# Another written order for TensorE's groups of matmuls (ORDER and LINE) in a four-layer transformer kernel

## The chip, the cores and the metric

The kernel runs on one core of one Trainium2 chip. A core has four compute engines that run side by side, each through its own list of instructions: TensorE (PE in the profile; its weight loads are listed apart as PEld), VectorE (DVE), ScalarE (ACT) and GpSimd (POOL). SyncE (SP) issues most of the transfers (DMA) between the chip's main memory and the on-chip memory. The engines wait for one another through semaphores.

The metric is the device time of one execution, in microseconds (us): 1479.94 before, the median of three runs (1478.99 to 1480.87). Lower is better.

## What is computed

Four layers are applied to 2048 tokens of width 448: A, B, A, B. A is an attention whose memory goes from segment to segment; B is a gated product (GLU). In short:

```python
def _A_ref(x, mem0, Wq, Wk, Wv, Wo, seg_len):     # seg_len 32, M 8 memory rows, 16 heads of 256
    mem = mem0
    for s in range(n_seg):                        # 64 segments
        xs = x[:, s * seg_len:(s + 1) * seg_len, :].copy()
        h = jnp.concatenate([mem, xs], axis=1)    # 40 rows
        q, k, v = ...                             # h times Wq, Wk, Wv
        p = _softmax(jnp.where(mask, q k / 16, -1e9))
        o = p v Wo
        mem = o[:, :M, :].copy()
        outs.append(o[:, M:, :])

def _B_ref(x, W_gate, W_up, W_down):
    gate = x W_gate
    h = gate * (gate > 0) * (x W_up)
    return h W_down

x = x + _A_ref(_layernorm(x), ...)
x = x + _B_ref(_layernorm(x), ...)
x = x + _A_ref(_layernorm(x), ...)                # the same weights again
x = x + _B_ref(_layernorm(x), ...)
```

The eight memory rows of a segment need those of the segment before it. So there is a recurrence of 63 steps in each A layer that can't be cut into parallel pieces.

## The kernel before, in words

**Weights first.** The kernel folds Wq with Wk into a matrix A and Wv with Wo into a matrix B, head by head. For this TensorE transposes the loaded weights (L864) and multiplies them (L880); the results go to A and Bsb. The code handles eight pairs of heads; the loads of each pair are issued on SP's queue (function `load`, with `weights` and `values` around it), those of Wq and Wk first, then those of Wv and Wo.

**The recurrence (`chain`, `middle`).** One pass of the main loop is a step; step n computes the memory rows of segment n of the first A layer and, seven steps behind (LAG = 7), those of segment n - 7 of the second. A step on TensorE is: memory times A (L1063), scores (L1296), then after the softmax on VectorE and ScalarE the transposes of the probabilities (L553 or L547), their product with the rows (L1357 and L1360), the product with B (L1107, in three groups; in the first two steps another form at L1200 to L1222), and the sum of the partial results with a selection matrix Sel (L533 with Sel, or L1139). Between these, VectorE, ScalarE and GpSimd take results out of the PSUM banks, split them in a high and a low part (Ohi and Olo, L1117 to L1122), turn them and write the next step's inputs.

**The rest fills in.** Everything else has slack: the 32 other rows of each segment, done for a tile of 128 tokens at a time (`att_group`: L1445 for the product with A, L1471 scores, L553 or L547 transposes, L1357 and L1360, then L533 or L537 for the product with B), the layer norms (`norm`, L1377 to L1390, transposes through L533), the GLU (`glu_units`, L1548 and L1577, and `glu_down`, through L533 or L537), and the stores. 

**How the order is made.** Every piece of work is an operation of a small planner, `_Sched`. Each has the engines that it may run on, a cost, what it reads and writes, and a priority. The planner goes through time, gives each engine its next operation and each result a PSUM bank (2 of pool C, 6 of pool G), and then writes the engines' instructions with the waits that the dependences need. Two strings steer it:

- LINE gives TensorE's order outright, for 2244 groups of matmuls. All groups stand in a list in program order; each sign is the place (0 to 79, and `~` adds 80) of the next group to take out of what is left:

```python
left = [o for o in self.ops if "pe" in o.engs]
...
out.append(left.pop(k + SIGNS.index(c)))
```

- ORDER holds a sign for each of 1132 parts of the program. It shifts the priority of that part's operations on the other engines and on SP's queue, in quarters of a step from -6.5 to +6.5:

```python
self.shift = 0.25 * (STEPS.index(ORDER[self.unit]) - 26) if self.unit < len(ORDER) else 0.0
```

Operations of the recurrence (level 0) are not shifted. Among the operations that could start, an engine takes those of the recurrence first and then the one with the lowest shifted time.

Three things follow from TensorE's order. Some groups have more than one form (`also`): the product with B and the down product of the GLU as full-array matmuls or in four strips of 32 columns (L533 or L537), transposes as full-array matmuls or in two row halves (L553 or L547). `line` picks the form that a group's neighbours have. A group whose form differs from the one before it is a turn. And where the planner sees TensorE idle for over 300 ns, `filler` puts matmuls that compute nothing used (L1613).

Of the kernel before, what the change touches and what calls it, by code (L numbers as in the profile page):

```python
# [32 lines left out]
ORDER = ("ICaaaaOUrUDzaqcLWBFvhKAQmXFbHJff0ZK0wA0bEK0NDJXhjQmlgNYQnskhcpNJDHZNZngWZTjmcjBAjxHSSfuazSiaMjVabyVardZaAxxvaa"
         "EaYgAaJrzaDcdaw0soaarpGhuNovjusPpyoeuyUBGJkuJFzJGx0tKaaacQaiNFmxXLyHxb00ADnzLBabRixTkKxGdaJXaIoicaqRaeuGFjpisL"
         "FcxuhjeZZv0CLUpBgeqL0egdRFyA0DaAAadPinsdymSWAiFrACcmGYxLcpcHvEYPmNEhvSTxPGnUaKl0PoPFoZjqPpXLmLLkPtatKanladLuBM"
         "vVacjOdMMa0bRkhDsXuevuhUWgFWUJjUAIAdYtapPaptYXDbGqNwcqAMiufAdvneygyexTpgEuIzKOjduGyWNv0dwbjgkuWyUPgaklsRtAapJZ"
         "SBaaxZazOryqpAViKovTklti0IkpHXIpCHjQFzEEzebgLcvAjkpGFaDHaoQGQc0xvLbnoJCpyUSXNrfYKuOeUuuOjUmQKAumJrdwbUtRGmfffc"
         "uZuF0NBYiiXwpK0pkpazCaxgSLIcYopEQzmNdxygZUdLlXHALQIuiGnZXcucuuLAWQVJavJahWrFbhnXTYBHOyHywgrOLPvYdBDuTsQyjlJrcR"
         "ZkxHGgVdoexoYmXmVBcxcGGhdcIbXxMsmaXBaoDGpL0GYgLn0SAPPyaQPdHWVJAIRjxdQGQOS0UXKlgtyObaEhaPtvBWTAJIoDZelscyxSCcds"
         "ndERVDSsrqvXOgYAswzuiyvgPiSf0UWjJuZHdBTrcN0fuOZyanhaIkEz0EsdGNyptHWTl0SiWCcQdqUiDEGQNYAlfmbPcLiwZoalTarMGlVdZb"  # L40
         "DLaVgRUWmanPhdttSUYlvNDDVxsTNNBcavVfpUveDiBzVtXxHjIREbnnpTzkYpcaYRaDmZaeaLlWPNozCKEe0SKUdfTzAxPrxdTEKbDqBfBXyx"
         "saANaasOtPpFycdVRiQYBzqmpHFQwUAWWepGzOGyGrRGIzIKYmpfzie0jHVsWhwCfuCtIAqAy0reaggzaMaoen0arBEurDaaaaaaTlneKDPaaa"
         "aaaaaaaaaaaaaaaaPEcWONgzaTGfZbfY")
# [55 lines left out]
class _Sched:  # L99
# [107 lines left out]
    def line(self):  # L207
# [1541 lines left out]
```

## Time and profile before

| | |
|---|---|
| median of three runs | 1479.94 us |
| lowest and highest | 1478.99 and 1480.87 us |
| the profiled execution | 1480.49 us |
| its span, first to last instruction | 1478.7 us |
| granted TensorE clock | 1.000 |
| DMA, mean over the span | 23 GB/s |
| in the first two fortieths of the span | 279 and 149 GB/s |

How to read the profile. One execution is taken by the hardware profiler. Times are microseconds unless marked ns. A row of a group or of the order in time names the line of the code (often a helper's: all results taken out of PSUM by `copy_any` have L523 or L526, all transfers L821), the engine, the operation, the tile written and the tiles read (buffer numbers are left out, so psG stands for any bank of pool G), the shape, and how many instructions were merged (x). In the rows in order of time the first two numbers are the start and the length; what stands in brackets is the engine's idle time before it and what ended that. A row of a wait names who waited for whom, the total, how often, and the longest. A row of busy times by stage has the stage, its length, then for PE, PEld, DVE, ACT and POOL the busy time and the number of instructions, and last the granted clock, the share of the DMA engines, and GB/s. Matmuls are pipelined: one of 448 columns is listed with some 350 ns, while the next can start 189 ns after it. So a busy PE is not a PE at its peak, and how closely matmuls follow is read from their starts.

### The profile page before, as it was taken

What the parts mean: (1) busy time and instruction counts of PE and PEld (TensorE: products, weight loads), DVE (VectorE), ACT (ScalarE), POOL (GpSimd) and SP (SyncE); (2) the same over time, 40 slices, a digit from 0 to 9 for tenths busy, and PEclk for the clock granted to TensorE, in tenths of its full rate; (3) what the DMA queues carried; (4) which work ended last, traced back from release to release, by engine and by line L of the source; (5) the groups of instructions that cost most, each with busy time, mean ns of one, the idle gap of its engine ahead of it and who ended that gap; (6) DMA issues with size and microseconds to landing.
All of it is one profiled execution on the core that took longest, in us unless ns stands there. A gap on an engine that the chain in (4) does not pass through costs nothing.

```text
span 1478.7 us, 82785 instructions
## 1 busy us (share of the span) xinstructions
PE 1467.1 (99%) x36957; PEld 1044.7 (71%) x36957; DVE 1131.3 (77%) x3703; ACT 909.4 (62%) x2632; POOL 175.7 (12%) x681
## 2 busy tenths in 40 slices
PE   9999999999999999999999999999999999999999
PEld 6656766777767776777768667677668676777676
DVE  7657778788878778687877778588876878788775
ACT  7775666676656656565656657466655656565543
POOL 3011111111111111011110111011110111011000
PEclk9999999999999999999999999999999999999999
DMA  9402100000000000000000000000000000000000
GB/s 279 149 26 71 51 8 9 8 9 8 9 5 14 9 14 9 3 19 5 18 5 14 9 14 9 4 18 5 16 6 14 7 11 12 5 11 5 11 6 15
DMA packets 62260, 34.09 MB, mean 23 GB/s; under 512 B 31808, under 2 KB 61776, under 8 KB 61904
## 3 DMA queue, kind: packets, MB, share of 16 engines
q1 hardware_dynamic: 61584, 28.54, 7.6%
q8 instruction: 290, 4.75, 1.3%
q14 instruction: 66, 0.54, 0.1%
q10 hardware_dynamic: 320, 0.26, 0.1%
HBM read 21.36 MB, written 1.84 MB: 16 GB/s over the span
## 4 chain that ended last, share of the span: by engine, by line
PE 96%; DVE 2%; ACT 1%; DMA 0%; issue 0%; SPq 0%; POOL 0%
PE psG L533 17%; PE psG L1445 17%; PE psC L1107 9%; PE psG L1548 9%; PE psC L1063 7%; PE psG L537 6%; PE psG L1063 5%; PE psG L1107 3%; PE psG L880 3%; PE psG L1357 3%; PE psG L1577 3%; PE psG L1471 3%; PE psC L1357 1%; PE psC L1296 1%; PE psG L864 1%; PE psC L1445 1%
## 5 line engine op out<-in xcount | busy, mean ns | idle before, releaser
L1445 PE MATMUL psG<-HT,A 64*128 64x128 bf16 x4932 | 279.5, 216 | 1.2 <-issue 1.1
L1445 PE MATMUL psG<-HX,A 64*128 64x128 bf16 x3699 | 262.1, 216 | 0.0
L1445 PEld LDWEIGHTS psG<-HT,A 64*128 64x128 bf16 x4932 | 231.0, 94 | 12.8 <-issue 5.2
L533 PE MATMUL psG<-Bsb,P 128*128 128x448 bf16 x909 | 194.2, 353 | 0.0
L1445 PEld LDWEIGHTS psG<-HX,A 64*128 64x128 bf16 x3699 | 191.3, 94 | 0.2 <-issue 0.2
L523 ACT ACTIVATE Ug<-psG 64x128 bf16<-64x128 f32 (+2 forms) x433 | 152.3, 370 | 55.4 <-PE psG L1445 43.3
L1280 DVE STREAM_TRANSPOSE uT<-Usb 128x384 bf16<-128x384 bf16 x280 | 144.5, 536 | 0.0
L1107 PE MATMUL psC<-Bsb,YTm 128*32 128x448 bf16 x2800 | 142.3, 353 | 0.1
L1063 PE MATMUL psG<-A,mT 64*32 64x448 bf16 x4088 | 134.3, 350 | 0.3 <-issue 0.2
L1548 PE MATMUL psG<-GG,glu 64*128 64x256 bf16 x2324 | 133.8, 269 | 0.0
L526 DVE CAST Ug<-psG 64x128 bf16<-64x128 f32 (+2 forms) x278 | 116.6, 429 | 17.9 <-PE psG L1445 12.3
L1063 PE MATMUL psC<-A,mT 64*32 64x448 bf16 x3752 | 125.8, 350 | 0.3 <-DVE mT L526 0.3
L533 PEld LDWEIGHTS psG<-Bsb,P 128*128 128x128 bf16 x909 | 78.7, 97 | 64.7 <-issue 5.6
L1548 PEld LDWEIGHTS psG<-GG,glu 64*128 64x128 bf16 x2324 | 110.1, 94 | 16.4 <-issue 1.9
L523 ACT ACTIVATE P<-psG 128x448 bf16<-128x448 f32 x207 | 106.6, 545 | 9.1 <-PE psG L1360 8.0
L1107 PEld LDWEIGHTS psC<-Bsb,YTm 128*32 128x32 bf16 x2800 | 71.2, 97 | 55.2 <-DVE YTm L526 0.7
L526 DVE CAST P<-psG 128x448 bf16<-128x448 f32 x148 | 89.2, 614 | 8.8 <-PE psG L1360 7.9
L1063 PEld LDWEIGHTS psC<-A,mT 64*32 64x32 bf16 x3752 | 62.1, 92 | 46.4 <-DVE mT L1145 4.4
L1063 PEld LDWEIGHTS psG<-A,mT 64*32 64x32 bf16 x4088 | 69.1, 92 | 30.2 <-issue 2.5
L526 POOL COPY HR<-Rsb 8x96 bf16<-8x96 bf16 (+1 forms) x132 | 37.2, 281 | 438.7 <-ACT Rsb L523 336.7
L1558 ACT ACTIVATE P<-psG 128x512 bf16<-128x512 f32 x83 | 49.4, 596 | 61.4 <-PE psG L1548 51.8
L1559 DVE TENSOR_TENSOR P<-P,psG 128x512 bf16<-128x512 bf16 x83 | 56.6, 682 | 36.4 <-ACT P L1558 36.1
(283 smaller groups left out, 3192.8 us busy)
## 6 DMA issues: line engine op xcount, KB each, us to landing
HR<-xn SPq DMA_DIRECT2D x128, 32.0 KB, 1.9
Tsb<-Rsb SPq DMA_DIRECT2D x256, 1.5 KB
Tsb<-Rsb SPq DMA_DIRECT2D x256, 2.0 KB
Bsb<-in_A_Wq_dram SPq DMA_DIRECT2D x6, 384.0 KB, 6.5
Bsb<-in_A_Wk_dram SPq DMA_DIRECT2D x6, 384.0 KB, 5.3
HR<-Rsb SPq DMA_DIRECT2D x126, 1.5 KB
HR<-Rsb SPq DMA_DIRECT2D x126, 2.0 KB
X<-in_A_x_dram SPq DMA_DIRECT2D x16, 112.0 KB, 3.8
```

The lines of the kernel that those rows point to most:

```text
L523: return E.activation(out, i, ACT.Copy, scale=1.0 if scale is None else scale)
L526: return E.tensor_copy(out, i)
L533: return E.matmul(out, lhsT=lhsT, rhs=rhs, **k)
L537: i = E.matmul(out[q], lhsT=w, rhs=rhs, tile_position=(0, 32 * j), **k)
L1063: i = E.matmul(ub[v].ap()[32 * j:32 * j + 32, 0:D], lhsT=self.mT[rw, WHERE[b], first:first + 32], rhs=cols, start=(b == 0), stop=(b == 6), ...
L1107: x = E.matmul(bk.ap()[32 * j:32 * j + 32, c0:c0 + d1 - d0], lhsT=self.YTm[:, q, :], rhs=self.Bsb[:, chunks[q], d0:d1], start=(i == 0), st ...
L1280: self.s.add("dve", 560, busy=486.0, fn=lambda E, e, q=q, of=of: E.transpose(outs[:, q], of), r=[("Usb", 2 * half + v, g) for v in vs for ...
L1357: return E.matmul(ps[:, n * q - off:n * q + n - off], lhsT=HR[rows, 128 * q:128 * q + 128], rhs=PT, start=True, stop=True, tile_position=( ...
L1445: i = E.matmul(ub[v].ap()[:, 128 * n:128 * n + 128], lhsT=self.A[rw, b, a0:a0 + 128], rhs=HT[rw, WHOLE[b], :, 0:SEG] if CROSS[b] is None e ...
L1548: i_ = E.matmul(two[v].ap()[:, 256 * c:256 * c + 256], lhsT=self.Wgu[rw, b, f0:f0 + 128], rhs=self.GG[rw, :, WHOLE[b] if CROSS[b] is None ...
L1558: s.add("act", ev_cost(512)["act"], lambda E, e, dst=dst, z=z: E.activation(dst, z(0), ACT.Relu), r=[two[0]], w=w, room=old)
L1559: s.add("dve", dv_cost(512), lambda E, e, z=z, dst=dst: E.tensor_tensor(dst, dst, z(1), ALU.mult), r=[two[1]], w=w)
```

## The change

Both strings are replaced, and nothing else. Both LINE strings place 2238 groups and leave the last six to program order; the old one has six `~` among its signs, the new one four. The functions that read the strings, the operations with their costs, tiles and dependences, the forms a group may have, and the buffers are the same. The first steps follow an older order, and the rest was searched on from there by the same rules. The two strings begin and end so:

```diff
-ORDER = ("ICaaaaOUrUDzaqcLWBFvhKAQmXFbHJff0ZK0wA0bEK0NDJXhjQmlgNYQnskhcpNJDHZNZngWZTjmcjBAjxHSSfuazSiaMjVabyVardZaAxxvaa"
...
-         "aaaaaaaaaaaaaaaaPEcWONgzaTGfZbfY")
+ORDER = ("wNaaaakeXaHRFRltlLTThvTInfRKLKSbzAOjIyTuXpvkWFDhFTTBurfhuDrlyVNFIDsnQWCkUOrPojWEKoQnmZqxjvoaVOjaaTQaApoaBNphaa"
...
+         "aaaaaaaaaaaaaaaanJmDaNxRaMcLybRh")
...
-LINE = ("AAAACAKABAIHAFEBBBAAHHAADABBABAIHBDAABAAAAIHBBBABAAAAIHHCFAACBAAH*HCDAABAABAIHCFBDAAAJAAKHGBDDABAAFIAhAddAcABA"
...
-         "APWJDDIHKAAANADFAFEABAEAAHDCAAAAADCBFAHEFEAD")
+LINE = ("AAAACBKBBIIACCBCBAAAHHEFBBBBABAJIBEAACBABAHICDCCAAAAAJHABBBCBABAIHCFBCCAAAAHIDFCABAAJBAHJBEFEBAAAAfjgAffACFABA"
...
+         "WEIDIHAJAAAACKECADCAKADADCAAAAADBBFAGEEEEE")
```

The signs of ORDER for the loads of Wv and Wo, for the eight pairs in the code's order (parts 82 to 89), are shifts of -4.75, -2, -2, 1.25, 5, 0, 6.25, -2 before and -2.5, 3.25, 3, -0.25, 4, 5.75, 2.25, 5.25 after.

More of the change, by code (lines that the diff above doesn't have):

```diff
@@ L32 @@
 STEPS = "ABCDEFGHIJKLMNOPQRSTUVWXYZabcdefghijklmnopqrstuvwxyz0"
-ORDER = ("ICaaaaOUrUDzaqcLWBFvhKAQmXFbHJff0ZK0wA0bEK0NDJXhjQmlgNYQnskhcpNJDHZNZngWZTjmcjBAjxHSSfuazSiaMjVabyVardZaAxxvaa"
[L34 to L42, printed above, removed]
-         "aaaaaaaaaaaaaaaaPEcWONgzaTGfZbfY")
@@ new lines @@
+ORDER = ("wNaaaakeXaHRFRltlLTThvTInfRKLKSbzAOjIyTuXpvkWFDhFTTBurfhuDrlyVNFIDsnQWCkUOrPojWEKoQnmZqxjvoaVOjaaTQaApoaBNphaa"
+         "baXiTaivDaCZCaVPHdaaEGAvjNKtOdjPUuqaByLiWIhuYTZmDL0NkaaaFDaoOlOvXSnPFy0neYWFLBLyAcxcIdoOLaBGRvMANasraKTJPRpHb0"
+         "LLxi0HhOZycEIBpvAGiwEexrCniStBahPaEiEwFdiUDNsiBHRItmfgNUqpidqNDnhNBXegTYhwdcjylLTrTWoUglJwXohXglKGadLaBJGGzuUq"
+         "umucUAYHyaNkmvvDoj0EXhOlceFAUIBHnxTxKmaISaKvxOVbdZfEjqAFnLAACtYuOgPGsSRGRcTWKzjXoKCSbm0y0JqHpudEhCUaTqlXrADaeT"
+         "PFaatDaLpVnhpsqRiqvGymkG0DzzgbIrcSGBzutzKergZXdAAkuwxaATaRkAvY0KoBAeoRPfzcSDUmGgKoTNxVeqyAXQdAHwePLiKUzVOkcNfT"
+         "QewM0KJS0pXspOrYneaJlaAEbPOcKXdujzVzSrggFoWsQXfYwRjQFehKXsuFhxxfP0g0aBVarnIxThVNLxiHlXpJugbMXQkYmhFjnRHyyTJPcp"
+         "JggyASVpNKfxemnARIrxSUcVecolCIkVSagzaFlRwd0cA0iS0LdEpPan0GRSVMmqvHRxVNgOt0NbOjYtunKaAdahtjVQThbpfVZxorrOxUjzik"
+         "nXCqWaIlzlmXigQEacgwayTSQXfB0BuaSfZtqfZkcIsWfxSYaZNamzWzHEDngEIpGzBpS0JSKAzQEVCvXXQPsPAkfGdbnnaNvgaYSauDeYtduW"
+         "qDQVQauMUadmViHtahFCelfuPTsgNkRZePkLpICYvMEzzzgxDjBiNxqnqGR0YRgafSaoEbmTatQl0JoTRTGL0krpWkTlAjGfWEjfXbPqmTjZdp"
+         "iaURawQryepunYDqRfqSKxqfVkrdwZAieIyRYIRyLrqMTQmyUmGKxTE0ZdpSehGHwM0thAtsFwTwaCVFaqXeNF0LgMriIiaaaaaabLmNKToaaa"
+         "aaaaaaaaaaaaaaaanJmDaNxRaMcLybRh")
@@ new lines @@
+SIGNS = "ABCDEFGHIJKLMNOPQRSTUVWXYZabcdefghijklmnopqrstuvwxyz0123456789+-*/=<>()[]{}.,:;!"
+LINE = ("AAAACBKBBIIACCBCBAAAHHEFBBBBABAJIBEAACBABAHICDCCAAAAAJHABBBCBABAIHCFBCCAAAAHIDFCABAAJBAHJBEFEBAAAAfjgAffACFABA"
+        "ZTAqXAEMASSA~VAQAPAlOABALAAZJCAKAGGAFBAaVAC-CABAWaFBEADPAECMDAEQLKAAESEOOOADEKDAIDCABBDABAAXAAAMADAAAHVNASaAFX"
+        "AFENHAAAEEHMBAZFYYYY>FIWAAUATFFRRRAAPAROOOAAALAAJoJvJAIIAHBJGGGAAEAACABAAAAXAAOUaAAAAWKdAJaJMRAWMAKHAAAJEJIAZD"
+        "AXXXXCCCUaCEABQACOAAQMMMAAKAKKKKJx5QJA1IIDLHHHAGGGGGGABEAJDACAAAAABRABAANTAAAXWAcJGASIAGVJAFAAGFDDAFAJZZZZBDAC"
+        "AETAAXRCCPAANNNOAALALLLL87LAQvJJCIBHHHIAGGGGGGfAFAKADACAAEAAACAAOUAAAAXeeKVLKAZSM}vMdAcAqKAAFAEEHASDA33FkECzGA"
+        "BYBuzAtlCjCGoooAAmAEVDmkkUAgAMflBBVcBAaZ7IYYYILAVCKVVVJAASAAANUOAMMgGLLLMjGGJAKLKbUJAPXIdHbHiHNAXKAKKJFFFAADDr"
+        "rrFQFFDmAUMGoAhAFf;EHdddAAbAcdcFEAAAXVAAUZTTAARRR4AQtSSSBEEBAAALAAAGHMAGFgFFFIAFADAABODBBZYRLnBVKzKZBYBLtLLBBB"
+        "FQKBEJI)>>BDDAC-CCECA6-X5AccBB000AAyAA0yyQvcRtbsATwgAAnDmqDckkkHDiJAgAAeeeWAAHALYeAAAVEDxYwTGlWGjGQQQAAOAOOOGL"
+        "AcKATJPEcIbIiMIIIAAGAzzzZFBQ2vADATrDCpAoooE~ConBnnnADkCAioADAfCCdAEbbbAAZZIDCXXXAAAbUAARRvRlRRRARnRGAABAAAJAAV"
+        "AaAfTelUkFAbhAFDDNzACLNLCAKBzJMBBBFFBGhGnBPA+++CjcGC5-CC3ABA0rBAxxxAAvAwwwld1stAbPGooDsnAmmmAmAKKiCFghgAKAdVOh"
+        "Awava2aaaCCYCAAYYYEoDAcUdjUAEQAPEjOpOoDNNNAALEKAI222EUDGAxRA1EVtAsDDApppFp~CpoCFElllCASiFAADDjdAFAFZEAAWWWAAUA"
+        "AATTTzrASYvEBQOEAMMCAAAIIIAAAFAAAAYBQCkcjPECCXMMCbU6BBwB2LBBBJIoLBEJJ>(>BDoDACe>H8CCLAB3B2AjBByyyAAwAAwwwcjAtb"
+        "yq;PqFo}oOCmmmnAMkAjljjBChMmAfAeAAAbbbAAZCFEbZZCVWAAEaTbAARAPPGBBMMMAAKCtJI777IOO-4ANBA0AAZxQDvvvDDMGrAsssRGFI"
+        "ouAlAMjj!Gi,GGgggAAAdAeeecAEAAYDCWAAATAAWRmRRRAhRGCCBAALAJAAVAAAAXAQABiiODBBLVUBKZKBKPBJ0JBBBFFBGADDA=<=DmCdc9"
+        "FCAg-ZA3u2lC000AAyFgAxxxAeARtAqQ;pp,pQsAnnnBCBlkCOAiiiAAffAAAcAgHaRHYYYAAWCYZYXNUCAAARACAUOVNNaCMMMBULADRJpI44"
+        "4EdHDAzFAA2DvOuVDsssAAqArrrpJoAnCHAMpjAiA<ADfffAAdBBEAbbbDDAAAUVAATASRvumAUQQQAEADAMAAJEAWcACCCAAQlRQZZTfTXCPR"
+        "zyBDBBLtPLBSO3B2BLIBBBFFBAsGDA555FfEC1CWC4CxABAuWRRrrrs~GRqAARopoBEmscbkCjA<AgAjAieeeEEcGbbbASACXCABBTYASAsADP"
+        "PPnEDNAPPPFNeXAKJKQAIlIcIaEDGGGAkGHFAFFvttAEGApAAtnIAlNDCiiiAAgDIeAgeed{DCAaEAAXcCWCAUUUAASAASSyqZARmGDPNCMMBL"
+        "LLABAIAdWAGAAnnSEdEjQaQEEXRAAABAMM1AsAyAAAKEEADA==hGFC+eABF*6BAE3mD111XAAzyFAxxAAAVtbQrhppQsAYsmmmDBBjPChlkAgA"
+        "hqnBeEeAccAbbbcAAAYYFPFYYAWHAAaTRAZJQZAOO4SOOOQExONAWV8CATZADAYQCGOvOOOAAMFLOOAFEIKAAIGBFFAEEEAEACAQBAdJHASAQA"
+        "WEIDIHAJAAAACKECADCAKADADCAAAAADBBFAGEEEEE")
```

19 lines of the change are left out of this document (removed).

## The prediction

> **What bounds the kernel now.** I read the page first, then the busy time by stage, then TensorE's own waits, then three places in order of time.
>
> ```profile
> span 1478.7 us, 82785 instructions
> PE 1467.1 (99%) x36957; PEld 1044.7 (71%) x36957; DVE 1131.3 (77%) x3703; ACT 909.4 (62%) x2632; POOL 175.7 (12%) x681
> ```
>
> TensorE (PE) is busy for 1467.1 of 1478.7 us, so 11.6 us are idle in all. The change adds and removes no matmul of the computation. What it can win is the idle time, the filler matmuls that the planner writes where it foresees a gap, and the cost of going from one tile form to another. The stages say where this lies (the second number is PE's busy time):
>
> ```profile
> 0.00:100.00 100.00, 96.55 (x1588) 61.22 (x1588) 66.28 (x158) 75.94 (x150) 20.00 (x62) 1.00 0.57 161
> 100.00:200.00 100.00, 98.77 (x2503) 67.60 (x2503) 75.00 (x257) 61.39 (x192) 13.43 (x54) 1.00 0.19 52
> 200.00:310.00 110.00, 108.39 (x2950) 75.72 (x2951) 88.50 (x305) 72.39 (x227) 17.71 (x73) 1.00 0.05 10
> 310.00:500.00 190.00, 189.99 (x5069) 136.98 (x5066) 153.61 (x520) 118.28 (x358) 22.17 (x87) 1.00 0.04 9
> 500.00:1000.00 500.00, 499.57 (x13193) 362.84 (x13187) 384.18 (x1279) 308.44 (x921) 56.43 (x222) 1.00 0.05 11
> 1000.00:1479.00 479.00, 473.83 (x11679) 340.38 (x11672) 363.76 (x1189) 272.98 (x788) 45.93 (x183) 1.00 0.04 10
> ```
>
> The first 310 us hold 3.45 + 1.23 + 1.61 = 6.3 us of idle time, the next 690 us only 0.01 + 0.43 = 0.4, the last stage 5.2. Of the last stage some 3 us are the end itself, which the order of groups can't reach: the last DVE addition starts at 1475.78, and a store follows.
>
> ```profile
> 1474.54 2.22 SPq L821 DMA_DIRECT2D out_dram<-X  x2
> 1475.78 0.62 DVE L1530 TENSOR_TENSOR X<-psG,X 128x448 bf16<-128x448 f32 x1 [1.27 <-PE psG L533]
> ```
>
> ```profile
> PE psG L880 <- ACT Bsb L523: 1.4, 5, 0.4
> PE psG L1445 <- issue: 1.1, 2, 0.8
> PE psC L533 <- DVE Olo L1122: 0.6, 2, 0.3
> ```
>
> PE's own waits are short and spread: 1.4 us on weight products, 0.6 us in the recurrence, and 1.1 us of "issue", in which it waited for nothing that the profile shows. The granted clock is 1.00 in every stage. So PE streams at full rate nearly everywhere, and one rewritten order can't be far from another.
>
> **The change part by part.** Each sign of LINE is the place of the next PE group in the list of those left, in program order. I read both strings off against that list of 2244 groups. 897 stand at the same place, half of all have moved by one place at most, one in ten by five or more. What every group computes is the same. Four things come out.
>
> *Tile forms.* Neighbours of unlike form (full array, four strips, two row halves and so on) are 543 before and 538 after. The price of a turn is in this stretch, which serves below too; it is step 10 of the recurrence:
>
> ```profile
> 235.15 1.12 PE L1107 MATMUL psC<-Bsb,YTm 128*32 128x448 bf16 x20
> ...
> 236.32 0.54 ACT L1117 ACTIVATE Ohi<-psC 128x448 bf16<-128x448 f32 x1 [0.54 <-PE psC L1107]
> ...
> 236.55 0.40 PE L533 MATMUL psG<-ident,xn 128*128 128x128 bf16 x4
> ...
> 236.79 0.73 PE L1613 MATMUL psG<-A 128*128 128x448 bf16 x3
> ...
> 236.90 0.62 DVE L1118 TENSOR_TENSOR Olo<-psC,Ohi 128x448 bf16<-128x448 f32 x1
> ...
> 237.56 0.20 DVE L1122 COPY Olo<-Olo 128x128 bf16<-128x128 bf16 x1
> ...
> 237.81 0.19 PE L533 MATMUL psC<-Sel,Ohi 128*128 128x32 bf16 x1 [0.29 <-DVE Olo L1122]
> ...
> 238.00 0.18 PE L533 MATMUL psC<-Sel,Olo 128*128 128x32 bf16 x1
> 238.11 0.09 PEld L1357 LDWEIGHTS psC<-PTr,HR 40*128 40x128 bf16 x1
> ```
>
> Eight 32-column matmuls start 237.81 to 238.00, 27 ns apart; the next group, of another form, loads at 238.11, so 0.11 us after the last start in place of 0.027: some 0.085 us a turn. Five turns fewer: **-0.4 us**. This holds under any cover, since PE pays it itself. Also 110 in place of 114 groups are in the four-strip form; its columns stream as long as the full form's (L1107 above: 20 matmuls in four strips in 1.12 us, that is five rounds of 0.19 and the pipeline's end), so nothing.
>
> *Step 10.* Here the step's last weight product (L1107) ends streaming near 236.1, ScalarE and VectorE make the high and low part of its sum (236.32 to 237.76), and only then can the Sel group start, at 237.81: a delay of 1.70 us. Before, 0.3 us of work stands between them, then three fillers (L1613) from 236.79. From 236.79 to 237.81 lie 1.02 us without useful work, and 0.23 before the xn transposes: 1.25 us. After, a group of 56 L1445 matmuls stands there, and the transposes behind it. Its price:
>
> ```profile
> 242.37 2.84 PE psG L1445 x98
> ```
>
> 29 ns each, so 1.62 us, and a turn: 1.7 to 1.8, just what the wait needs. The filler and the wait go: **-1.25 us** (0 if the L1445 group's own inputs came late, which no row here shows).
>
> *Step 1.* The same, among the weights' products:
>
> ```profile
> 77.41 0.27 PE L1296 MATMUL psC<-HT,uT 128*128 128x40 bf16 x4
> 77.52 0.35 PE L1613 MATMUL psG<-A 128*128 128x448 bf16 x1
> 78.24 0.55 PE L880 MATMUL psG<-P,glu 128*128 128x448 bf16 x2 [0.36 <-ACT Bsb L523]
> 78.99 0.23 PE L553 MATMUL psC<-ident,Pm 128*128 128x64 bf16 x2 [0.20 <-DVE Pm L1314]
> 79.42 0.55 PE L880 MATMUL psG<-P,glu 128*128 128x448 bf16 x2 [0.20 <-ACT Bsb L523]
> 79.91 0.34 PE L1357 MATMUL psC<-PTm,HR 40*128 40x128 bf16 x3
> ```
>
> By starts: 0.72 us from 77.52 to 78.24, then two matmuls of 0.19 and 0.37 lost to 78.99, then two of 0.03 and 0.37 lost to 79.42: 1.46 us. After, 42 L1445 matmuls (1.22 us) stand between the scores (L1296) and the transposes (L553), and the product that waited goes elsewhere. The softmax takes 78.99 - 77.52 = 1.47, of which 0.1 to 0.2 is left uncovered. **-1.3 us**; what is late next is the L1357 group, by about 0.1.
>
> *Step 9.* The change goes the other way here. The transposes L553 and their consumer L1357, with an L1445 group of 42 between them before, now stand side by side. Elsewhere that hop is seen without cover to spare:
>
> ```profile
> 429.37 0.22 PE L553 MATMUL psC<-ident,Pm 128*128 128x64 bf16 x2
> 429.62 0.22 ACT L523 ACTIVATE PTm<-psC 104x64 bf16<-104x64 f32 x1 [0.89 <-PE psC L553]
> 430.00 0.34 PE L1357 MATMUL psC<-PTm,HR 40*128 40x128 bf16 x6
> ```
>
> 0.63 us from start to start, less 0.06 of L553's own: **+0.57 us**. Queued behind it on PE are a GLU group and the next L553, which nothing else makes up for.
>
> Sum of what I can place: -0.4 - 1.25 - 1.3 + 0.57 = -2.4 us. Against it stands what I can't: an order that removes lates makes others, among queues of ScalarE and VectorE that I don't see. The covers of the common hops (L553 to L1357, L1107 to the Sel group, and so on) are about as short in one order as in the other, so a group is about as likely to come late. Bounds: none new (0), or as much again as all the idle time of the first 310 us (+6.3). I take +0.9, a third of the 2.55 relieved, because it is nearer to the short waits of the rows above than to a second stage's whole idle time. **Net -1.5 us.** The profiled execution took 1480.49 us (its span and 1.8 around it), 0.55 above the median of 1479.94; the difference put on the median gives **1478.4 us**.
>
> The "issue" gaps I leave as they are. [...]
>
> **Rivals.** *The relief stays and little comes anew (faster).* For it: the places above are exact, and the 690 us in the middle show that an order can leave 0.4 us idle. Then -2.4, with the 1.1 us of issue and part of the 1.4 us on L880 gone: -4.0, 1475.9.
>
> *Weights come late (slower).* ORDER also sorts the loads on SP's queue. The signs put the eight pairs of Wv and Wo in the order 0, 3, 6, 2, 1, 4, 7, 5 (by place in the code's list), where pair 1 was second. Its transposes (L864) stand seven places further down on PE, past the four L1063 groups of step 0, by the matmul counts some 4.4 us.
>
> ```profile
> GB/s 279 149 26 71 51 8 9 8 9 8 9 5 14 9 14 9 3 19 5 18 5 14 9 14 9 4 18 5 16 6 14 7 11 12 5 11 5 11 6 15
> Bsb<-in_A_Wv_dram SPq DMA_DIRECT2D x4, 384.0 KB, 6.4
> Bsb<-in_A_Wv_dram SPq DMA_DIRECT2D x8, 32.0 KB, 5.7
> P<-in_A_Wo_dram SPq DMA_DIRECT2D x3, 448.0 KB, 7.4
> 25.50 1.76 SPq L821 DMA_DIRECT2D Bsb<-in_A_Wv_dram  x3
> 47.15 1.06 PE L864 MATMUL psG<-ident,Bsb 128*128 128x128 bf16 x16
> ```
>
> A pair is 384 + 64 + 448 KB, 0.92 MB. The first starts at 25.50; four pairs ahead and 6.4 us to land must be over by 47.15 + 4.4 = 51.5. At the first slice's 279 GB/s a pair takes 3.3 us, and pair 1 lands at 45.1: no wait. At the second slice's 149 it takes 6.2, and it lands at 56.7, 5.2 us late: 1483.6. It decides below 0.92/4.9, 187 GB/s. Against it: that slice's mean counts the time after the last load, and semaphores may keep SP from the written order.
>
> *It does nothing.* Lates moved, none gained beyond the turns: -0.4 or so, 1479.5. This and my forecast fall together within the bound below.
>
> **How the numbers follow.** A change of this kernel's time under 0.2%, 3.0 us, can hardly be told from none. Forecast and "nothing", within 1477.0 to 1482.9: 0.45. Relief alone, or relief elsewhere too, below 1477.0: 0.35. Late weights 0.14, and scattered lates near the +6.3 bound 0.06, above 1482.9: 0.20. The likeliest case's own range is 1476.9 to 1481.5. The range for all reaches to the relief with 2 us more (1473.9) and to the late weights (1483.6): 1473.5 to 1484.0.
>
> **What would show it.** In the changed profile: no L1613 row near step 10 and an L1445 group before its first Sel matmul; an L1445 group between L1296 and L553 in step 1; PE's idle time before L1357 in step 9 near 0.57; PE idle in the first 310 us 4 to 6 us in place of 6.3, and under 1 us from 310 to 1000. Late weights would show as PE waiting for a DMA between 45 and 60 us. I am wrong if the middle 690 us gain more than 1.5 us of idle time, or if the first 100 us change by more than 2 us.

## The result, and the profile after

The changed kernel takes 1477.18 us (median of 14 runs, 1476.22 to 1478.09), the kernel before 1480.33 (14 runs, 1478.99 to 1481.37). The ratio is 0.9979, with a 95% interval of 0.9971 to 0.9987. That is 3.15 us less, which this interval tells from no change. Forecast were 1478.4 us and -1.5 us. The change is about twice the forecast one; the times lie closer because the kernel before is 0.4 us slower in these 14 runs than in the three that the forecast started from.

The profiled execution took 1478.07 us, and its span is 2.5 us shorter than that of before. The page, and the busy times by stage (stage, length, then busy time of PE, PEld, DVE, ACT and POOL; last the granted clock, DMA share and GB/s):

```profile
span 1476.2 us, 82695 instructions
PE 1465.7 (99%) x36911; PEld 1043.6 (71%) x36911; DVE 1127.7 (76%) x3723; ACT 905.1 (61%) x2610; POOL 175.9 (12%) x683
```

```profile
0.00:100.00 100.00, 97.51 (x1582) 61.15 (x1582) 68.81 (x169) 74.42 (x148) 20.34 (x64) 1.00 0.55 161
100.00:200.00 100.00, 99.19 (x2541) 68.52 (x2541) 74.32 (x254) 61.63 (x193) 13.89 (x54) 1.00 0.19 52
200.00:310.00 110.00, 108.06 (x2967) 75.74 (x2969) 86.80 (x305) 73.17 (x232) 18.59 (x76) 1.00 0.05 10
310.00:500.00 190.00, 189.10 (x5060) 136.47 (x5057) 150.14 (x514) 120.84 (x354) 20.63 (x82) 1.00 0.04 9
500.00:1000.00 500.00, 498.83 (x13119) 361.81 (x13111) 387.73 (x1296) 300.03 (x898) 56.22 (x223) 1.00 0.05 11
1000.00:1477.00 477.00, 472.99 (x11672) 339.86 (x11666) 359.86 (x1188) 275.05 (x790) 46.29 (x185) 1.00 0.04 10
```

TensorE is idle 2.49 + 0.81 + 1.94 = 5.2 us in the first 310 us (6.3 before), 0.90 + 1.17 = 2.1 in the next 690 (0.4 before), and 4.0 in the last stage (5.2 before). Part of the gain is not idle time at all: the fillers (L1613) near 7, 77 and 237 us are gone, and a filler counts as busy. From each one's start to the next group's start, they took 0.96 + 0.71 + 1.03 = 2.7 us before.

PE's waits (who waited for whom: total us, times, longest):

```profile
PE psG L1445 <- issue: 1.0, 2, 0.6
PE psG L1357 <- DVE PTm L526: 0.7, 1, 0.7
PE psC L1063 <- issue: 0.5, 1, 0.5
PE psG L1471 <- issue: 0.4, 1, 0.4
PE psG L880 <- ACT Bsb L523: 0.4, 2, 0.3
PE psC L533 <- DVE Olo L1122: 0.3, 1, 0.3
```

The waits on the weight products (L880) fell from 1.4 to 0.4 us, those in the recurrence (L533 on Olo) from 0.6 to 0.3. New is 0.7 at L1357, in step 9. "Issue" is still there, at other groups.

Where the time went is read best from the groups' starts. The same groups stand in both orders, so both traces can be asked when a given amount of TensorE's work was done. The difference (after minus before), summed from the start:

```
near, us of before    44    66   102   147   212   223   257   312   353   884   936  1459
difference, us      -0.1  +0.6  -0.6  -1.3  -1.6  -0.5  -1.6  -1.4  +0.0  -0.6  +0.2  -2.3
```

Step 9 (212 to 223) costs 1.1 and step 10 (223 to 257) gives 1.1. By 312 us the new order is 1.4 ahead, loses all of that by 353, and is 2.3 ahead near the end. The swings behind 312 us are for the most part at places of "issue", and the experiments turned on them.

### The profile page after: what moved, and what is told of

Same layout as the page of the kernel before. It is cut to its first block, busy times and chain, and to the rows that moved or that the text cites. A ratio compares the mean times of both kernels' runs of the same rounds, so it can differ in the third digit from the quotient of the medians.

```text
span 1476.2 us, 82695 instructions
## 1 busy us (share of the span) xinstructions
PE 1465.7 (99%) x36911; PEld 1043.6 (71%) x36911; DVE 1127.7 (76%) x3723; ACT 905.1 (61%) x2610; POOL 175.9 (12%) x683
## 3 DMA queue, kind: packets, MB, share of 16 engines
q8 instruction: 290, 4.75, 1.3%
## 4 chain that ended last, share of the span: by engine, by line
PE 96%; DVE 2%; ACT 1%; SPq 1%; issue 0%; DMA 0%; POOL 0%
PE psG L1445 17%; PE psG L533 16%; PE psC L1107 10%; PE psG L1548 9%; PE psC L1063 7%; PE psG L537 6%; PE psG L1063 5%; PE psG L880 3%; PE psG L1357 3%; PE psG L1577 3%; PE psG L1107 3%; PE psG L1471 2%; PE psC L533 2%; PE psC L1296 1%; PE psC L1357 1%; PE psG L864 1%
## 5 line engine op out<-in xcount | busy, mean ns | idle before, releaser
L1445 PE MATMUL psG<-HT,A 64*128 64x128 bf16 x4968 | 282.5, 216 | 0.1
L1445 PE MATMUL psG<-HX,A 64*128 64x128 bf16 x3726 | 264.5, 216 | 1.0 <-issue 1.0
L1445 PEld LDWEIGHTS psG<-HT,A 64*128 64x128 bf16 x4968 | 233.2, 94 | 11.8 <-issue 3.6
L1445 PEld LDWEIGHTS psG<-HX,A 64*128 64x128 bf16 x3726 | 193.0, 94 | 1.3 <-issue 1.3
L523 ACT ACTIVATE Ug<-psG 64x128 bf16<-64x128 f32 (+2 forms) x458 | 161.1, 369 | 51.5 <-PE psG L1445 34.7
L533 PE MATMUL psG<-Bsb,P 128*128 128x448 bf16 x862 | 184.9, 353 | 0.0
L1107 PE MATMUL psC<-Bsb,YTm 128*32 128x448 bf16 x2968 | 150.6, 353 | 0.0
L1063 PE MATMUL psG<-A,mT 64*32 64x448 bf16 x4116 | 134.7, 350 | 0.1
L1063 PE MATMUL psC<-A,mT 64*32 64x448 bf16 x3724 | 126.4, 350 | 0.9 <-issue 0.5
L526 DVE CAST Ug<-psG 64x128 bf16<-64x128 f32 (+2 forms) x271 | 110.7, 419 | 14.9 <-PE psG L1445 10.0
L523 ACT ACTIVATE P<-psG 128x448 bf16<-128x448 f32 x222 | 113.0, 545 | 10.0 <-PE psG L1360 7.2
L533 PEld LDWEIGHTS psG<-Bsb,P 128*128 128x128 bf16 x862 | 74.2, 97 | 61.7 <-issue 6.3
L1107 PEld LDWEIGHTS psC<-Bsb,YTm 128*32 128x32 bf16 x2968 | 75.7, 97 | 57.5 <-ACT YTm L523 0.7
L1063 PEld LDWEIGHTS psC<-A,mT 64*32 64x32 bf16 x3724 | 62.3, 92 | 49.0 <-DVE mT L1145 5.1
L526 DVE CAST P<-psG 128x448 bf16<-128x448 f32 x140 | 84.8, 614 | 11.1 <-PE psG L1360 10.5
L1063 PEld LDWEIGHTS psG<-A,mT 64*32 64x32 bf16 x4116 | 69.2, 92 | 28.4 <-ACT mT L523 1.5
```

The source lines that it names most:

```text
L523: return E.activation(out, i, ACT.Copy, scale=1.0 if scale is None else scale)
L526: return E.tensor_copy(out, i)
L533: return E.matmul(out, lhsT=lhsT, rhs=rhs, **k)
L1063: i = E.matmul(ub[v].ap()[32 * j:32 * j + 32, 0:D], lhsT=self.mT[rw, WHERE[b], first:first + 32], rhs=cols, start=(b == 0), stop=(b == 6), ...
L1107: x = E.matmul(bk.ap()[32 * j:32 * j + 32, c0:c0 + d1 - d0], lhsT=self.YTm[:, q, :], rhs=self.Bsb[:, chunks[q], d0:d1], start=(i == 0), st ...
L1445: i = E.matmul(ub[v].ap()[:, 128 * n:128 * n + 128], lhsT=self.A[rw, b, a0:a0 + 128], rhs=HT[rw, WHOLE[b], :, 0:SEG] if CROSS[b] is None e ...
```

## Experiments

Times are given as ratios to runs of the kernel before on the same chip, with 95% intervals, since its median differs by 1 us between groups of runs (1480.3 to 1481.3). Orders are read off LINE as a list of groups: line, number of matmuls.

### One place alone

Step 10's relief alone, and step 1's alone, each on the kernel before.

```diff
 L1357 x10
-L1445 x56
 L1445 x42
 L1296 x8
...
 L553 x2
+L1445 x56
 L533 x4
 L533 x8
```

> The kernel before with one group moved: the L1445 group of 56 matmuls that stood ahead of step 9's scores (210.7 us) is put behind step 10's last weight product (L1107) and the transposes, ahead of xn's (L533) and the Sel group. Theory A (the prediction: the move relieves step 10): step 10 gains 1.25 us, and step 9 pays nothing that it names: 1480.3 - 1.25 = 1479.1. Theory E (cover only moves: the 1.57 us of work taken from step 9 leaves a wait there of about the same size, by the fillers planned there 0.4 to 1.1 us): step 10 gains 1.0 to 1.25, step 9's scores or softmax wait 0.6 to 1.2 us more, in all 0 to -0.4 us: 1480.1.

```diff
 L1296 x4
+L1445 x42
 L880 x2
 L553 x2
...
 L1357 x5
-L1445 x42
 L1107 x20
```

> The kernel before with one group moved: the L1445 group of 42 matmuls that stood behind the L1357 group at 101.8 us is put behind step 1's scores (L1296, 77.4 us). Theory A (the prediction): step 1 gains 1.3 us and nothing is said of the place that it came from: 1479.0. Theory E (cover only moves): step 1 gains 0.8 to 1.2 us, and at 102 us the L1107 group or what stands ahead of it waits 0.5 to 1.2 us more: in all 0 to -0.4 us, 1480.1.

Measured: step 10 alone 1.0005 (0.9996 to 1.0014), no gain; step 1 alone 1.0015 (1.0006 to 1.0024), some 2 us slower. The filler at step 10 is gone, as is the one at 77.5 us. But in order of time (start, length, engine, line, tile written and read) the first kernel has, at step 9, with the scores that the moved group had covered:

```profile
212.22 0.55 PE L1613 MATMUL psG<-A 128*128 128x448 bf16 x2
212.96 0.36 PE L1296 MATMUL psC<-HT,uT 128*128 128x40 bf16 x8 [0.18 <-DVE uT L1280]
...
247.78 0.35 PE L1613 MATMUL psG<-A 128*128 128x448 bf16 x1
```

and the second, behind step 1 and at the place that its group came from:

```profile
80.18 0.73 PE L1613 MATMUL psG<-A 128*128 128x448 bf16 x3
81.30 0.55 PE L880 MATMUL psG<-P,glu 128*128 128x448 bf16 x2 [0.39 <-ACT Bsb L523]
...
103.78 0.36 PE L1613 MATMUL psG<-A 128*128 128x448 bf16 x1
104.46 1.32 PE L1107 MATMUL psG<-Bsb,YTm 128*32 128x448 bf16 x24 [0.31 <-ACT YTm L523]
```

The time in fillers rose from 6.4 us to 7.1 and 8.0. In step 1 the covered softmax was not even last: the product behind it (L880) waits for its evicted weights (Bsb) all the same. A group of L1445 is cover, and where there is no spare group, relieving one place uncovers another. For step 10 Theory E holds. For step 1 cover explains only a part. In its trace 0.85 us are lost before 66 us, where nothing was moved, some 0.5 between 66 and 110 us, and 3.1 behind 110 us, where both orders are the same; of these, waits for instructions make up 2.3 (6.7 against 4.4, below). The profiled execution was also the slowest of the 11. Nor is this move the whole trade of the change: the new order has a group of 56 at the place near 102 us again, and one group fewer in step 0 (that of 56 at 58.49 us before).

### The early half and the late half

Up to group 505 (about 304 us) and from there on, the two orders hold the same groups, so each can be continued with the other. In short (the kernel has the joined strings written out):

```diff
-LINE = OLD_LINE
+LINE = NEW_LINE[:505] + OLD_LINE[505:]
-ORDER = OLD_ORDER
+ORDER = NEW_ORDER[:262] + OLD_ORDER[262:]
```

(505 counts places: a sign with the ~ before it is one.)

> The new order for the first 505 of TensorE's groups (to about 304 us) and the first 262 places of ORDER, the old order for all behind. Theory I (the gain lies in the fillers and waits of the first 310 us; what the traces show behind that is chance of the fetch): the ledger of the first 310 us, -1.4 to -1.5, so 1480.4 - 1.5 = 1478.9, or with the start's part lower, 1478.5 to 1479.3. Theory J (half of it lies behind 310 us): 1478.8 as well here, but the next kernel tells them apart.

The other way round:

> The other half: the old order for the first 505 groups and 262 places, the new order behind. Theory I: only the turns of that part and chance, 1480.4 - 0.3 = 1480.1. Theory J (a later part with fewer dense runs of small matmuls waits less for its instructions in the mean): the traces' ledger there, -0.9, or what is left of the -3.15 beside the early half, -1.6: 1478.8 to 1479.5.

Measured: early half new 0.999 (0.9981 to 0.9999), late half new 0.9982 (0.9973 to 0.9991); the whole new order, beside them on the same chip, 0.998 (0.9971 to 0.9988). Of 1481 us that is -1.5 and -2.7; together they are more than the whole's -3.0, which the intervals allow. The early half agrees with the ledger's -1.4 at 312 us. The late half carries about as much or more, which the prediction did not see at all: Theory J.

### What the late half waits for

In the kernel before, the longest "issue" wait stands in the middle of a group of L1445 (a number in brackets is idle time, with what ended it):

```profile
1143.89 0.23 PE L1445 MATMUL psG<-HT,A 64*128 64x128 bf16 x2 [0.80 <-issue]
```

In the changed kernel the rows near 313 us show a group of 16 that stops after three matmuls:

```profile
312.76 0.37 PE L1296 MATMUL psG<-HT,uT 128*128 128x40 bf16 x8
312.97 0.23 PE L1471 MATMUL psG<-HT,Ug 128*128 128x40 bf16 x3
313.57 0.48 PE L1471 MATMUL psG<-HT,Ug 128*128 128x40 bf16 x13 [0.37 <-issue]
```

No tile comes new at the fourth. From the page, the larger of its two queues of the kind "instruction":

```profile
q8 instruction: 290, 4.75, 1.3%
```

4.75 MB over 290 packets is 16 KB a packet. The trace holds 74290 instructions of TensorE (36911 matmuls, as many weight loads and 468 others), that is 256 to a packet of this queue, and 127 matmuls (36911 over 290). And the two go together in time: when instruction 256k + 192 starts, k packets have landed, at 577 of 580 places in this trace and that of before. So I take this queue to load TensorE's program. Theory A below is that PE waits at packet boundaries, after stretches in which small matmuls use up instructions faster than they come.

First, the same stream with more instructions ahead (each 448-column filler as seven of 40 columns):

```diff
+            if ns > 100:
+                n, x = 7 * n, self.A[:, 1, 0:40]
             for _ in range(n):
                 i = E.matmul(self.psum[bank][:, 0:x.shape[1]], lhsT=w, rhs=x, start=True, stop=True)
```

> The changed kernel, with each filler matmul of 448 columns written as seven of 40 columns: the same time (7 x 27 ns for 190 ns), but 60 more matmuls, 120 instructions, in the stream by 301 us, so all later packet boundaries fall 60 matmuls earlier in the work. Theory A (fetch, in packets of 256 instructions): the wait inside the L1471 group near 313 us, after its third matmul, leaves that place and stands 60 matmuls earlier, at about the 27th matmul of the L1445 group near 310.6 us; that near 317.7 moves to the 30th matmul of the L1445 group before it, that near 898 to the 26th matmul of an L1063 group; their sizes may change; time 1477.2 within 1.5 us. Theory B (the wait belongs to the group, by its inputs or its bank): it stays after the third matmul of the L1471 group, and the time stays at 1477.2.

In its trace the L1471 group runs through, and the wait stands inside the L1445 group that starts at 315.30, after its 30th matmul:

```profile
315.30 0.23 PE L1445 MATMUL psG<-HT,A 64*128 64x128 bf16 x2
...
316.03 0.28 PE L1445 MATMUL psG<-HT,A 64*128 64x128 bf16 x4
316.76 0.23 PE L1445 MATMUL psG<-HX,A 64*128 64x128 bf16 x2 [0.45 <-issue]
```

This place was foretold to the matmul: 60 earlier in the work, the same count in the stream (7322). The other two places foretold, near 310.6 and 898 us, show no wait of 0.25 us or more in this profile. The time was missed: 0.9995 (0.9986 to 1.0004), some 2 to 3 us slower than the changed kernel, with more such waits (4.8 us behind 304 us in this profile, 3.8 in the changed kernel's). So in this run moving the boundaries was not free.

Second, two fillers more, one ahead of the wait, one where none follows soon:

```diff
-                n = int((t0 - free[e] - 300.0) * 0.8 / ns)
+                n = 3 if done in (516, 538) else int((t0 - free[e] - 300.0) * 0.8 / ns)
```

> The changed kernel with two more fillers of three 448-column matmuls (0.57 us each): one ahead of the L1296 group near 312.8 us, just before the wait in the L1471 group, and one ahead of an L533 group near 328 us, which no such wait follows for 13 us. Theory A (fetch): the first is absorbed, since the fetch goes on under it: the L1471 group's inner wait of 0.55 falls to about 0, and the groups behind come 0 to 0.15 us later; the second costs its 0.57 us, less what it saves of the 0.3 us near 341 us. In all +0.3 to +0.7: 1477.7. Theory B (a wait of the group itself, or chance): both cost 0.57 us: +1.1, 1478.3.

Its rows at the first place:

```profile
312.51 0.74 PE L1613 MATMUL psG<-A 128*128 128x448 bf16 x3
313.09 0.36 PE L1296 MATMUL psG<-HT,uT 128*128 128x40 bf16 x8
313.30 0.56 PE L1471 MATMUL psG<-HT,Ug 128*128 128x40 bf16 x16
```

The group runs through. The three fillers also move the packet boundary to the group's start, and the packet had landed 1.9 us before that. Against the changed kernel's trace the groups behind the first filler come 0.56 us later and 0.53 of it is back two groups on; a further 0.52 is won at the next wait (near 317.7). The second filler costs 0.57, and 0.30 is back at 341 us. So 1.14 us of useless work cost nothing that the runs can tell: 0.9973 (0.9964 to 0.9983), where both theories had expected some loss. The wait at 313 us is not in every profile (below), so one trace does not prove the repayment; that nothing was lost over nine runs supports it.

Third, the changed kernel once more:

> The changed kernel once more, unchanged, for a second profile of the same stream. Theory A with chance in the size (TensorE's stream is refilled in packets; the places of possible waits are fixed by the count of instructions, whether and how long it waits there differs from one execution to the next): inner waits only at the matmul counts 7195, 7322, 7958, 20691, 22604 of the first profile, or at others that are a multiple of about 127 matmuls away from these, with other sizes; all other waits (0.35 us at L880 near 52 us, 0.90 at step 9, 0.24 and 0.31 near 295 and 300 us) the same within 0.02 us. Theory H (all is fixed): the same waits with the same sizes. Time 1477.2 within 0.5.

Its second profile has the same dependence waits (0.35 us near 52, 0.90 at step 9, 0.24 and 0.31 near 295 and 300), while the inner waits differ in size and some in place. Counting the matmuls that started before each inner wait (one inside a group, 0.25 us or more), over these kernels and those of the next sections, these counts came up most often:

```
matmuls before it   seen in, us
 7195 to  7197      after 0.53, again 0.31, step 1 alone 0.48
 7322               after 0.51, again 0.30, short fillers 0.61, no fillers 0.65, late half 0.58
 7449 to  7451      short fillers 0.49, no fillers 0.65, step 1 alone 0.54, early half 0.28
20309 to 20312      before 0.50, again 0.91, four places 0.90, filler ahead 0.45, step 1 alone 0.60, early half 0.61
20691 to 20694      before 0.25, after 0.69, step 1 alone 0.52, early half 0.36
28840 to 28842      before 0.97, step 10 alone 0.42, step 1 alone 0.74, early half 0.55
28968 and 28969     before 0.35, step 10 alone 0.90, early half 0.26
```

Different orders, the same counts, about 127 or a multiple of it apart: in these traces the places go with the packets. Which of them wait, and how long, is partly chance (the wait at 20309 is 0.91 us in one profile of the changed kernel and under 0.25 in the other). So Theory A holds with chance in the size, and B and H fall.

The traces show it more directly, since they hold the arrival of each program packet. Take the twelve profiles of this and the other sections but for "One string without the other", behind 100 us, and count all of TensorE's recorded instructions (matmuls, weight loads, semaphore instructions). All 66 inner waits of 0.25 us or more stand at instruction 192 or 193 of a run of 256, and each ends 1.2 to 1.6 us after a packet has landed; at all packet boundaries together the median is 3.1 us. So, in these profiles, what such a wait is for is the next packet of the program.

A boundary can also fall at the start of a group, and then the profile may put the wait down to another engine. In the kernel before, one such wait stands at a packet boundary, 1.54 us after a packet landed:

```profile
1399.16 0.34 PE L1357 MATMUL psG<-PTx,HR 40*128 40x128 bf16 x6 [0.84 <-ACT Usb L523]
```

The weight loads of the same group stop with it, for "issue". The changed kernel has no wait there, and its lead grows by 0.8 us.

The chance in these waits has a mean, and the order changes it. Waits at groups that hold a packet boundary, over 0.1 us, summed behind 304 us (a group's time from its start to the next start, less the lower quartile of its kind):

```
old order there:  before 4.4, step 10 alone 4.9, step 1 alone 6.7, early half 4.1         mean 5.0
new order there:  after 3.8, again 2.6, late half 2.2, no fillers 2.7, filler ahead 1.6,
                  short fillers 4.8                                                       mean 2.9
```

2.1 us less in the mean, though one profile of the new order (short fillers) lies among those of the old. Against it stands a new wait for VectorE of 0.25 to 0.3 us behind the L1360 group near 1141.5 us, in both profiles of the changed kernel. The waits came most often after dense stretches. In the twelve profiles, of the boundaries whose last two packets passed in under 7.5 us (14.6 ns an instruction) 73 of 333 waited (over 0.1 us), from 7.5 to 9.1 us 61 of 997, and over that 30 of 2066. The kernel before has 34 stretches under 7.5 us, the changed one 30 and 28 in its two profiles. At 73 waits in 333, four to six stretches fewer are about one wait fewer, an estimate that makes up a part of the 2.1 us; where the rest comes from stays open.

### Putting old stretches back, and spreading

```diff
 L1063 x24
+L1063 x32
 L1063 x56
-L1063 x32
...
 L1357 x10
+L1445 x42
 L1445 x56
-L1445 x42
...
```

> The changed kernel, with the groups of four stretches (516 to 519, 521 to 570, 1277 to 1278 and 1396 to 1397 in the written order; about 313 to 349, 820 and 897 us) put back in the old order. Theory A (TensorE's idle time there is instruction fetching: its stream comes in packets of 16 KB, 256 instructions, and a dense stretch of small matmuls empties one before the next is there): the waits of 0.5 to 0.9 us inside the groups near 313, 316, 341, 821 and 897 us go, or shrink as in the kernel before; by the shift of the groups' starts between the two traces that is 1.43 + 0.44 + 0.72 = 2.6 us, so 1477.2 - 2.6 = 1474.6. Theory B (such waits fall anywhere in any execution, by chance): they come up at other places and the time stays at 1477.2, within 1 us.

Measured: 0.997 (0.9959 to 0.9981), 1476.5 us. Of the 2.6 us that the ledger promised, some 1.3 came (0.997 beside 0.9979, overlapping intervals). In its profile the waits near 313 to 341 us are gone and that near 897 us is 0.28 in place of 0.77. But 0.90 stands at 809 us, which the changed kernel's first profile happened not to have. A ledger of two single traces had taken chance for a difference of the orders.

Nine more groups moved by 2 to 9 places (and their neighbours by one), two of them here:

```diff
 L1063 x56
-L1357 x10
 L1577 x56
 L1577 x56
+L1357 x10
...
 L1063 x56
+L533 x4
 L1471 x16
 L553 x4
-L533 x4
```

> The kernel with four old stretches, with nine groups more moved by 2 to 9 places so that fewer runs of two packets (512 instructions) pass in under 7.5 us. Theory A: fewer chances for a wait, by the planner's times and the mean wait of such runs in the eight profiles 0.3 us less than with the four stretches alone: 1476.2. Theory H or B: 1476.5 or, where the moved groups come late, more.

Measured: 0.9968 (0.9957 to 0.998), 1476.8 us. It and the last one are the lowest ratios of all, but their intervals overlap the changed kernel's, so no version is shown to beat it.

### Without the fillers

```diff
-                n = int((t0 - free[e] - 300.0) * 0.8 / ns)
+                n = 0
```

> The changed kernel without its ten filler matmuls (L1613), which compute nothing that is used. Theory A, as the prediction counts them (a filler stands in time in which TensorE would wait anyway): the idle time takes its place, 1477.2 within 0.5 us, with the granted clock still 1.00. Theory C (fillers overshoot: they hold up a group that could start): up to 0.3 us a place faster, 1476.0. Theory D (without them the clock falls): slower by over 1 us and a granted clock under 1.00 behind the gaps.

Measured: 0.9986 (0.9977 to 0.9995), about 1 us slower than with them, with overlapping intervals. Idle time takes the fillers' place, and nothing starts sooner (Theory C falls). At one place the clock fell, by the busy time of TensorE in each microsecond (start:end, length, busy time and instructions, granted clock, DMA share, GB/s):

```profile
301.00:302.00 1.00, 0.33 (x4) 1.00 0.00 0
302.00:303.00 1.00, 0.70 (x18) 1.00 0.28 74
303.00:304.00 1.00, 0.81 (x26) 0.69 0.24 56
304.00:305.00 1.00, 1.00 (x28) 0.50 0.11 25
305.00:306.00 1.00, 1.00 (x32) 0.50 0.03 3
306.00:307.00 1.00, 1.00 (x36) 0.61 0.04 4
307.00:308.00 1.00, 1.00 (x64) 1.00 0.02 2
```

Behind 0.67 + 0.30 + 0.19 = 1.2 us of idle time within three, the granted clock is 0.50 to 0.69 from 303 to 307 us, and the first L1063 group there takes 2.53 us to the next one's start in place of 1.33, 1.2 us longer. Theory D holds for this place; after the gaps at the other three (0.85 to 1.08 us from one matmul's start to the next) the clock stayed at 1.00. Counting a filler as a wait is right to within this.

### One string without the other

```diff
-ORDER = ("ICaaaaOUrUDzaqcLWBFvhKAQmXFbHJff0ZK0wA0bEK0NDJXhjQmlgNYQnskhcpNJDHZNZngWZTjmcjBAjxHSSfuazSiaMjVabyVardZaAxxvaa"
+ORDER = ("wNaaaakeXaHRFRltlLTThTvInfRKLKSbzAOjIyTuXpvkWFDhFTTBurfhuDrlyVNFIDsnQWCkUOrPojWEKoQnmZqxjvoaVOjaaTQaApoaBNphaa"
...
```

> The kernel before with the new string ORDER alone (the order of the loads on SP's queue and of the work of ScalarE, VectorE and GpSimd); TensorE's order stays. Theory A (the gain lies in TensorE's order, the rest only follows it): no gain, and the new load order, with the transposes of pair 1 still early, leaves TensorE waiting for that pair near 45 us: by the planner's fillers there 2 to 3 us, and more waits in the middle, 1483 to 1490. Theory F (the gain lies in the other queues): 1477.5.

```diff
-LINE = ("AAAACAKABAIHAFEBBBAAHHAADABBABAIHBDAABAAAAIHBBBABAAAAIHHCFAACBAAH*HCDAABAABAIHCFBDAAAJAAKHGBDDABAAFIAhAddAcABA"
+LINE = ("AAAACBKBBIIACCBCBAAAHHEFBBBBABAJIBEAACBABAHICDCCAAAAAJHABBBCBABAIHCFBCCAAAAHIDFCABAAJBAHJBEFEBAAAAfjgAffACFABA"
...
```

> The kernel before with the new string LINE alone (TensorE's order); the loads and the other queues keep the old ORDER. Theory A (the gain lies in TensorE's order alone): 1477.2 to 1478.5. Theory G (the two strings only fit each other: the other queues serve TensorE's groups in the order of the old string, and loads of the pairs come in the old order): slower than both, with waits near 16 and 34 us for loads and at some places in the middle: 1483 to 1495.

Measured: 1.0126 (1.0111 to 1.0142) and 1.0105 (1.0091 to 1.0119), 19 and 16 us slower than before, more than any theory said. The first shows the late weights that the prediction had as a rival. With the new loads and TensorE's old order, pair 1 is not there when its transposes come up:

```profile
47.28 2.51 PE L1613 MATMUL psG<-ident 128*128 128x128 bf16 x42
50.53 1.07 PE L864 MATMUL psG<-ident,Bsb 128*128 128x128 bf16 x16 [0.74 <-DMA Bsb<-in_A_Wv_dram]
```

They could start at 47.28 and start at 50.53, 3.25 us late. In the new order these transposes stand some 4 us of other work further down, just enough. The rest of the loss is spread over the span: from each filler's start to the next group's, fillers took 18.4 and 15.4 us in these two, against 6.4 before. Neither string carries the gain; each is made for the other (Theory G).

## Why the prediction came out as it did

The time lay within the likeliest case's own range (1476.9 to 1481.5); the forecast was 1.2 us too high. The change itself, -3.15 us, was twice the forecast -1.5, and the reasons were right for about half of it.

- **Step 10, -1.25:** right in place and size. The L1445 group stands before the Sel matmuls, no L1613 is near. From L1107's start to the L1357 group behind Sel it was 4.66 us (233.45 to 238.11) and is 4.99 (231.17 to 236.16), with 1.57 of work more: 1.24 won. First the row of before that the prediction did not show, then those of after:

```profile
233.45 2.82 PE L1107 MATMUL psC<-Bsb,YTm 128*32 128x448 bf16 x56
```

```profile
231.17 2.82 PE L1107 MATMUL psC<-Bsb,YTm 128*32 128x448 bf16 x56
...
233.97 0.22 PE L1445 MATMUL psG<-HT,A 64*128 64x128 bf16 x2
...
235.63 0.19 PE L533 MATMUL psC<-Sel,Ohi 128*128 128x32 bf16 x1
236.16 0.23 PE L1357 MATMUL psC<-PTr,HR 40*128 40x128 bf16 x1
```

- **Step 9, +0.57:** the place was right, the size too small. I took the hop from another place, where ScalarE copies the transposes; here VectorE does. The row says 0.92 us from start to start, so +0.87, and L547 itself comes 0.2 late; PE's idle time before L1357 is 0.72, where 0.57 was named:

```profile
213.95 0.20 PE L547 MATMUL psC<-ident,Pm 64*128 64x64 bf16 x2
214.87 0.34 PE L1357 MATMUL psG<-PTm,HR 40*128 40x128 bf16 x6 [0.72 <-DVE PTm L526]
```

  The prediction added steps 9 and 10 to -0.7. They are one trade: the group that covers step 10 is the one that step 9 lost, and together the two come to about 0.

- **Step 1, -1.3:** right at its place. The L1445 group stands there, and L553 waits 0.1 as foretold:

```profile
76.80 0.27 PE L1296 MATMUL psC<-HT,uT 128*128 128x40 bf16 x4
77.00 0.23 PE L1445 MATMUL psG<-HT,A 64*128 64x128 bf16 x2
...
78.37 0.23 PE L553 MATMUL psC<-ident,Pm 128*128 128x64 bf16 x2
```

  From these scores (L1296) to 102 us the new order wins 1.2 us. But it comes to them 0.6 us late, work for work: step 0 has one group of 42 left, where it had groups of 42 and 56 (56.67 and 58.49 us) before. So the ledger from 44 to 102 us gives only -0.5. What failed here is that a relieved wait was counted in full without asking where the cover came from.

- **New lates, +0.9:** near. Placed for the first 310 us were about -2.2 (step 10, step 1, step 9 and part of the turns); the ledger has -1.4, so +0.8 came anew. It was a guess of a share, and the right sum hides that its parts (102 to 147 us, 0.7 won; the start, where the filler's 0.96 at 7 us gave way to other waits and only 0.1 was won) were not foreseen.

- **Tile forms, -0.4:** read off the strings; no run separates the price of a turn. The premise that no matmul is added or removed is off by 39: without the fillers the trace has 36901 in place of 36940, since some products in four strips now stand in one piece. The prediction gave that no price, and no run gives it one.

- **The issue gaps, left as they are:** this step failed. Behind 304 us the new order waits about 2.1 us less for its instructions in the mean, and the late half alone gives 0.9982. The row at 1143.89 was a hint that the step passed over: it shows PE waiting 0.80 us inside a group, for nothing that the profile names. In the traces such waits stand about 127 matmuls or a multiple of it apart, and came to 1.6 to 6.7 us in a profile behind 304 us, up to 0.97 at one boundary. The forecast -1.5 with the 1.1 us of issue won as well makes -2.6, nearer to the measured -3.15.

- **Signs named ahead:** idle time of 5.2 us in the first 310 us fits 4 to 6. Under 1 us from 310 to 1000 us does not (2.1), and the gain of 1.6 there passes the 1.5 at which I said I would be wrong. That sign was badly chosen: a single profile of that stage holds chance of that size (the second profile has 1.5). No wait for a DMA stands between 45 and 60 us, so late weights did not come, though with TensorE's order unmoved they would have.

Of the rivals, "relief stays and little comes anew" ended nearest in time (1475.9). That is in part luck: the waits for instructions that it counted are the true half, but the relief of steps 1 and 10 was in good part paid for at steps 0 and 9. "It does nothing" is refuted by the interval.

## What to carry to other kernels

Before counting a covered wait as won, follow the cover to the place it was taken from; where TensorE has no spare work, only the sum over both places counts. With 1% of idle time, look for waits inside a group that no tile explains, count the instructions before them, compare the counts between kernels, and look whether a program packet landed shortly before the wait ended (1.2 to 1.6 us in these traces). Differences of 1 to 2 us between two single traces of such a kernel need a second profile, or runs of one half at a time, before they are given a cause.

## What the runs showed of the hardware that was not expected

In the twelve profiles, behind 100 us, all 66 waits of 0.25 us or more inside a group, the longest 0.97 us, stood at TensorE's packet boundaries (packets of 16 KB, one to 256 recorded instructions), and TensorE went on 1.2 to 1.6 us after a packet had landed. They came most often after dense stretches: over 0.1 us at 73 of 333 boundaries where two packets passed in under 7.5 us, and at 30 of 2066 where they took over 9.1 us. The same boundary waited in one execution and not in the next (behind 20309 matmuls 0.91 us in one profile of the changed kernel, under 0.25 in the other). For one and the same late half the sums differ by 2 to 3 us between profiles (4.1 to 6.7 in the old order, 1.6 to 4.8 in the new); 28 runs of the kernel before spread over 5.0 us (1478.4 to 1483.4), and that these waits cause the spread is not shown. A filler of 0.57 us ahead of such a boundary was paid back in one trace (0.53 of 0.56 us two groups on). And in the kernel without fillers the granted clock was 0.50 to 0.69 from 303 to 307 us, behind 1.2 us of idle time between 301 and 304, and TensorE was busy for 3.81 of those four us.
